# A decode attention kernel with its TensorE program turned into a hardware loop over half heads

## The chip, the cores and the metric

The kernel runs on one core of a Trainium2 chip. The metric is device time in microseconds (us) of one execution. The change was measured with four runs of each kernel.

## The reference, cut to what matters

One token goes through a layer norm, then through attention with 16 query heads over 8 cached key and value heads, and beside it through a small gated feed-forward. The caches decide the cost: 65536 positions of 256 bf16 numbers, for 8 heads, keys and values, are 537 MB.

```python
B, Sq, D = 1, 1, 448
Hq, Hkv, Sk, Dh = 16, 8, 65536, 256
q = (x @ wq) split into 16 heads
scores = einsum("bhqd,bhkd->bhqk", q, k) * Dh ** -0.5      # two query heads per key head
p = softmax(scores);  o = einsum("bhqk,bhkd->bhqd", p, v);  A = o @ wo
# feed-forward: g = silu(x @ w_gate), u = x @ w_up, y = (g * u) @ w_down
out = x + A + (xn + y * sigmoid(r))
```

## The kernel before

Keys and values stream into a ring in SBUF in chunks of 64 positions per partition (128 x 64 x 256 bf16 = 4.19 MB, 32 KB per partition). The ring is a bump allocator: whatever comes next takes the next free stretch, and it also holds all weights. With 84480 elements it holds 5.2 chunks.

```python
RING = 84480
...
K_CHUNKS = [64] * 8
V_CHUNKS = [64] * 8
...
SPREAD = True
...
for n, it in enumerate(items):
    if pos + it["size"] > RING:
        pos = 0
    it["off"] = pos
    # it["need"]: the last earlier item that overlaps this stretch; the issue waits until it is free
...
def prog_sp():                       # one queue issues all loads, in order
    for n, it in enumerate(items):
        for m in range(max(0, it["need"] - 8), it["need"] + 1):
            wait("sp", "pe", ("FREE", m))
        ... nc.sync.dma_start(dst, src).then_inc(sem_it[it["sem"]], 16)
```

For each set of 16 positions TensorE transposes the keys (16 fp32-typed transposes, `ps_t`), VectorE and ScalarE copy them to SBUF, TensorE multiplies them with q (8 matmuls, `ps_q`), and the scores are transposed into place (`ps_s`). When a head is complete, softmax runs and its V chunks are multiplied with the probabilities (`ps_o`). The keys of the next head stream between them.

The gate weights of the feed-forward are loaded with a rearranged source. The rows land on partitions in another order, so a second set of activation columns exists to match.

```python
def flat_dma(src, n, off, spread):
    def d(a):
        dst = a[:, off:off + RP * n // 2]                # 128 partitions
        v = src.rearrange("a b -> (a b)")
        if spread:
            return dst, v.rearrange("(u a n) -> a u n", a=8, u=P // 8)
        return dst, v.rearrange("(p n) -> p n", p=P)
    return d
...
item("ffn1", RP * F, [flat_dma(B_w_gate, F, 0, SPREAD), flat_dma(B_w_up, F, RP * F // 2, False)])
```

The program of every engine is fully written out: TensorE executes 9576 matmuls, each with a weight load, and no branch.

Of the kernel before, what the change touches and what calls it, by code (L numbers as in the profile page):

```python
# [2 lines left out]

# [4 lines left out]
FP32 = mybir.dt.float32  # L8
# [4 lines left out]
RING = 84480  # L13
NSEM = 16
NTB = 4
NKT = 8
K_FIRST = [16, 16, 32] + [64] * 7
K_CHUNKS = [64] * 8
V_CHUNKS = [64] * 8
V_LAST = [64] * 7 + [32, 16, 8, 8]  # L20
SPREAD = True
WO_END = 2
ACT_M = (3,)
TORD = (3, 0, 1, 2)


def bass_parallel_sum__gqa_block_cached__moe_arch_mod__decode_kernel(
# [22 lines left out]
    HR = D // P  # L50
# [6 lines left out]
    NSET = NPP // SETN  # L57
    SBN = 256
    NSB = NPP // SBN
    SETS_PER_SB = SBN // SETN  # L60
    HB = FK // 2
    assert rep == 2 and NH == 2 and NPP % SBN == 0
# [6 lines left out]
    OROWS = 32 * (NG - 1) + 2 * rep  # L69

# [7 lines left out]
    ring = S_("ring", [P, RING], BF16)  # L78
    kt_buf = [S_(f"kt_buf{i}", [P, 8 * P], BF16) for i in range(NKT)]
    s2 = [S_(f"s2_{i}", [P, 512], BF16) for i in range(2)]  # L80
    S_sb = [S_(f"S_sb{i}", [P, NPP, rep], BF16) for i in range(2)]
    ident_bf = S_("ident_bf", [P, P], BF16)
# [6 lines left out]
    xe_row = S_("xe_row", [1, 2, 2, NE, P], BF16)  # L89
    xnT_sb = S_("xnT_sb", [P, 2, 2 * NE + 2 * (NE - 1)], BF16)  # L90
    qT_sb = S_("qT_sb", [P, NH, Hq], BF16)
    m1p = S_("m1p", [P, 2, rep, NSB], FP32)
    m1 = S_("m1", [P, 2, rep], FP32)
    gmax = S_("gmax", [rep, 1], FP32)
    diag = S_("diag", [rep, rep], FP32)
    negmax = S_("negmax", [P, Hkv, rep], FP32)
    rowsum = S_("rowsum", [P, Hkv, rep], FP32)
    rs = S_("rs", [P, Hkv, NH, rep], FP32)
# [4 lines left out]
    oT_sb = S_("oT_sb", [P, 2, NH, rep], BF16)  # L103
# [18 lines left out]
    ps_tf = [t[:, :].bitcast(FP32) for t in ps_t]  # L122
    ps_q = PS_("ps_q", [P, 512], FP32)
# [8 lines left out]
    sems = []  # L132

    def SEM(name):
        s = nc.semaphore(name)
        sems.append(s)
        return s.__enter__()

    sem_prog = {e: SEM(f"prog_{e}") for e in ("pe", "act", "dve", "pool")}
    sem_it = [SEM(f"sem_it{i}") for i in range(NSEM)]  # L140
    sem_w0 = SEM("sem_w0")
    sem_out = SEM("sem_out")
# [3 lines left out]
    class Ctx:  # L146
        emit = False
        ev = {e: {} for e in sem_prog}
        cnt = {e: 0 for e in sem_prog}
        waited = {}  # L150
        tasks = {"dve": [], "act": []}

    ctx = Ctx()

    def mark(e, key, ins):
        ctx.cnt[e] += 1
        c = ctx.cnt[e]
        if ctx.emit:
            assert ctx.ev[e][key] == c, (e, key, ctx.ev[e][key], c)
            ins.then_inc(sem_prog[e], 1)  # L160
        else:
            assert key not in ctx.ev[e], (e, key)
            ctx.ev[e][key] = c
        return c
# [5 lines left out]

    def wait(we, e, key):
        if not ctx.emit:
            return
        c = ctx.ev[e][key]
        k = (we, e)
        if ctx.waited.get(k, 0) >= c:
            return
        ctx.waited[k] = c
        engines[we].wait_ge(sem_prog[e], c)

    def wait_val(we, sem, val, key):
        if not ctx.emit:
            return
        k = (we, key)
        if ctx.waited.get(k, 0) >= val:
            return
        ctx.waited[k] = val
        engines[we].wait_ge(sem, val)

    def op(e, key, fn):  # L190
        mark(e, key, fn(engines[e]) if ctx.emit else None)
# [6 lines left out]
    items = []  # L198

    def item(kind, size, dmas, **kw):  # L200
        items.append(dict(kind=kind, size=size, dmas=dmas, **kw))
        return len(items) - 1

    def flat_dma(src, n, off, spread):
        def d(a):
            dst = a[:, off:off + RP * n // 2]
            v = src.rearrange("a b -> (a b)")
            if spread:
                return dst, v.rearrange("(u a n) -> a u n", a=8, u=P // 8)
            return dst, v.rearrange("(p n) -> p n", p=P)  # L210
        return d

    def kv_item(kind, src, h, n0, J):
        def d(a):
            return (a[:, 0:J * Dh].rearrange("p (j d) -> p j d", d=Dh),
                    src[0, h].rearrange("(p n) d -> p n d", p=P)[:, n0:n0 + J, :])
        return item(kind, J * Dh, [d], h=h, n0=n0, J=J)

    def wo_item(h):
        def d(a):  # L220
            return (a[:, 0:rep * NH * D].rearrange("p (i f n) -> p i f n", i=rep, f=NH),
                    A_wo[h * rep * Dh:(h + 1) * rep * Dh, :].rearrange("(i p f) n -> p i f n", i=rep, f=NH))
        return item("wo", rep * NH * D, [d], h=h)

    def head_chunks(kind, src, h, sizes):
        r, n = [], 0
        for J in sizes:
            r.append((kind, src, h, n, J))
            n += J
        assert n == NPP  # L230
        return r

    item("wq", RP * HqDh // 2, [flat_dma(A_wq, HqDh, 0, False)])
    ks = head_chunks("k", A_k_cache, 0, K_FIRST)
    for h in range(1, Hkv):
        ks += head_chunks("k", A_k_cache, h, K_CHUNKS)
    vs = []
    for h in range(Hkv):
        vs += head_chunks("v", A_v_cache, h, V_CHUNKS if h < Hkv - 1 else V_LAST)

    def v_next():
        v = vs.pop(0)
        if v[3] + v[4] == NPP and v[2] < Hkv - WO_END:
            wo_item(v[2])
        kv_item(*v)
        if v[2] == 0 and v[3] == 2 * V_CHUNKS[0]:
            item("ffn1", RP * F, [flat_dma(B_w_gate, F, 0, SPREAD), flat_dma(B_w_up, F, RP * F // 2, False)])
        if v[2] == 0 and v[3] == 3 * V_CHUNKS[0]:
            item("ffn2", FK * D, [lambda a: (a[:, 0:FK * D].rearrange("p (f n) -> p f n", f=2),
                                             B_w_down.rearrange("(f p t) n -> p f (t n)", p=P, f=2))])  # L250

    for n, k_ in enumerate(ks):
        kv_item(*k_)
        if n >= len(K_FIRST) + 1:
            v_next()
    while vs:
        v_next()
    for h in range(Hkv - WO_END, Hkv):
        wo_item(h)



    pos = 0
    live = deque()
    semtot = [0] * NSEM
    for n, it in enumerate(items):
        if pos + it["size"] > RING:
            pos = 0
        it["off"] = pos
        lo, hi = pos, pos + it["size"]  # L270
        need = n - NSEM
        for m in list(live):
            o = items[m]
            if o["off"] < hi and lo < o["off"] + o["size"]:
                need = max(need, m)
        while live and live[0] <= need:
            live.popleft()
        live.append(n)
        it["need"] = need
        pos = hi  # L280
        s = n % NSEM
        semtot[s] += 16 * len(it["dmas"])
        it["sem"], it["val"] = s, semtot[s]
        assert it["size"] <= RING

    def ap_of(n):
        it = items[n]
        return ring[:, it["off"]:it["off"] + it["size"]]

    def wait_item(we, n):  # L290
        it = items[n]
        wait_val(we, sem_it[it["sem"]], it["val"], ("it", it["sem"]))

    def free_item(n):
        alias("pe", ("FREE", n), ctx.cnt["pe"])

    def prog_sp():
        for n, it in enumerate(items):
            for m in range(max(0, it["need"] - 8), it["need"] + 1):
                wait("sp", "pe", ("FREE", m))  # L300
            for d in it["dmas"]:
                if ctx.emit:
                    dst, src = d(ap_of(n))
                    nc.sync.dma_start(dst, src).then_inc(sem_it[it["sem"]], 16)  # L304
        wait("sp", "dve", ("RES", Hkv - 1))
        if ctx.emit:
            nc.sync.dma_start(out[0], res_bf[:, :]).then_inc(sem_out, 16)
            nc.sync.wait_ge(sem_out, 16)

    def prog_pool():  # L310
# [23 lines left out]
        alias("pool", "CONST", ctx.cnt["pool"])  # L334


    st = dict(slot=0, m=[], pend_qk=None, pend_jt=None)
    deferred = deque()

    def slot():  # L340
        st["slot"] += 1
        if deferred and deferred[0][0] <= st["slot"]:
            deferred.popleft()[1]()

    def defer(after, fn, tag=None):
        deferred.append((st["slot"] + after, fn, tag))

    def flush():
        while deferred:
            deferred.popleft()[1]()  # L350

    def evac_T(e, g):
        wait(e, "pe", ("T", g))
        if g >= NKT:
            wait(e, "pe", ("QK", (g - NKT) // NG))
        kt, tb = kt_buf[g % NKT], ps_t[g % NTB]
        if e == "dve":
            op(e, ("EV", g), lambda x: x.tensor_copy(out=kt[:, :], in_=tb[:, :]))  # L358
        else:
            op(e, ("EV", g), lambda x: x.activation(out=kt[:, :], in_=tb[:, :], func=ACTF.Copy))  # L360

    def ev_engine(m):
        return "act" if m in ACT_M else "dve"

    def pe_T(n, s, m, j):

        g = s * NG + m
        if g >= NTB:
# [524 lines left out]
```

## Time and profile before

| | before |
|---|---|
| median of runs, first three / all four | 1312.85 / 1312.37 us |
| bytes read | 549 MB |
| rate in most slices | 430 GB/s |
| 549 MB at 430 GB/s | 1277 us |
| TensorE busy | 922.5 us, 70% |

First the page of the kernel before: the busy times with their share of the span, the rate in 40 equal slices of 32.8 us, and the DMA queues with their packets.

```profile
span 1310.5 us, 20912 instructions
...
PE 922.5 (70%) x9576; PEld 694.6 (53%) x9576; DVE 539.0 (41%) x895; ACT 432.4 (33%) x559; POOL 4.5 (0%) x34
...
GB/s 400 430 430 430 384 335 433 431 427 432 431 430 429 429 430 429 431 429 431 431 431 431 428 430 430 431 430 429 428 430 429 431 423 430 430 430 431 431 430 205
...
q1 hardware_dynamic: 22026, 549.04, 98.5%
q8 instruction: 75, 1.23, 0.4%
...
```

The first slice, the fifth and sixth and the last fall well short of 430 GB/s; the others stay within 2% of it. `q8` is instruction fetch: 75 packets of 16 KB, 1.23 MB, a fifth of a per cent of the bytes.

The table of waits, its line for TensorE and the K chunks (total us, times, longest):

```profile
...
PE ps_t L374 <- DMA ring<-in_A_k_cache_dram: 300.3, 55, 8.8
...
```

TensorE waits 300 us for keys, so the DMA is the limit.

The next view cuts the span into stretches around the gate load. Each line gives the stretch, its length, and each engine's busy time with its count of instructions; the last three columns are granted TensorE clock (as a share of full speed), busy share of the 16 DMA engines, and GB/s.

```profile
...
core 0: us, PE busy (x) PEld busy (x) DVE busy (x) ACT busy (x) POOL busy (x), PEclk, DMA share, GB/s
148.00:156.00 8.00, 4.80 (x29) 3.88 (x30) 2.08 (x3) 1.06 (x2) 0.00 (x0) 0.63 1.03 442
156.00:164.00 8.00, 7.98 (x84) 6.45 (x84) 5.28 (x9) 4.78 (x6) 0.00 (x0) 0.95 0.97 224
164.00:172.00 8.00, 1.90 (x32) 0.67 (x32) 0.39 (x1) 1.88 (x2) 0.00 (x0) 0.91 1.09 236
172.00:180.00 8.00, 0.00 (x0) 0.00 (x0) 0.00 (x0) 0.00 (x0) 0.00 (x0) 0.50 0.94 260
180.00:188.00 8.00, 5.32 (x98) 5.30 (x98) 0.00 (x0) 0.00 (x0) 0.00 (x0) 0.50 0.98 421
...
```

From 156 to 180 us the DMA engines are as busy as ever and move little more than half. The packets' own durations in the trace say how: 12544-byte packets (gate and up) take 0.94 us, and 0.47 us once it is over; the 32 KB packets of the caches that run at the same time take 2.34 us on average instead of 1.22.

The same view at the end:

```profile
...
1284.00:1292.00 8.00, 2.99 (x32) 0.80 (x24) 0.00 (x0) 0.00 (x0) 0.00 (x0) 0.71 0.83 343
1292.00:1300.00 8.00, 4.62 (x48) 1.24 (x48) 0.00 (x0) 0.00 (x0) 0.00 (x0) 0.69 0.35 137
1300.00:1308.00 8.00, 5.32 (x28) 1.31 (x28) 0.85 (x2) 0.00 (x0) 0.00 (x0) 0.52 0.08 32
...
```

The DMA engines run out one after the other: the busy share is 0.35 and then 0.08. From 1296 to 1305 us it is about 0.13, that is about two engines of 16 (0.13 x 16 = 2.1).

The last steps in the timeline (start, duration, engine, line):

```profile
...
1303.50 0.60 PE L694 MATMUL ps_o<-ring,S_sb 128*4 128x512 bf16 x4 [0.66 <-DMA ring<-in_A_v_cache_dram]
1304.90 0.27 PE L534 MATMUL ps_m<-sel_bf,ob_sb 100*128 100x2 bf16 x4 [0.80 <-DVE ob_sb L514]
1305.10 3.15 PE L562 MATMUL ps_s<-ring,oT_sb 128*1 128x448 bf16 x8
```

After the last four V matmuls only the output projections of the last two heads remain, and the span ends 7.0 us after they start.

One more table is needed; it comes from the trace's records of semaphore increments. For every whole chunk it holds 16 increments, at different times and as many as the page counts DMA engines; I read each as the landing of one engine's part. Listed is how many us before the last one each of the 16 came, for one item near the given time.

```
before,  254 us:  0.0 0.4 1.3 2.4 3.2 3.4 3.6 3.7 7.6 8.2 8.2 8.3 8.3 8.3 10.6 11.0
before, 1274 us:  0.0 1.2 7.8 8.6 8.7 9.3 9.4 9.5 9.6 12.3 14.9 15.2 15.2 15.5 19.0 19.5
```

The engines drift apart, and the kernel waits for the last of them.

### The profile page before, as it was taken

To read this page: it belongs to the slowest core of one execution; us is meant where nothing else is said; L and a number is where in the kernel's file an instruction comes from. 1 tells how busy PE (TensorE), PEld (TensorE's weight loads), DVE (VectorE), ACT (ScalarE), POOL (GpSimd) and SP (SyncE) were. 2 spreads that over 40 slices of the span, in tenths; PEclk is the share of its full clock that TensorE was granted. 3 is DMA by queue.
4 is the path that set the end of the run, shared out by engine and by line. 5 is a ranking of instruction groups with operands and counts; after the bars stand their busy time and mean duration, and the time that the engine had idled before them with its cause. 6 is when DMAs were issued, how large, how long until landed. Compare 5 with 4: busy or idle time off the path is not lost.

```text
span 1310.5 us, 20912 instructions
## 1 busy us (share of the span) xinstructions
PE 922.5 (70%) x9576; PEld 694.6 (53%) x9576; DVE 539.0 (41%) x895; ACT 432.4 (33%) x559; POOL 4.5 (0%) x34
## 2 busy tenths in 40 slices
PE   4998837768668577677677677577676686786534
PEld 4886625546546456455555556455465565565201
DVE  5776404444344344344343354344343353453200
ACT  2665303333233233233233243233332342332100
POOL 1000000000000000000000000000000000000000
PEclk9999768888888788787887888888887887888756
DMA  9999999999999999999999999999999999999994
GB/s 400 430 430 430 384 335 433 431 427 432 431 430 429 429 430 429 431 429 431 431 431 431 428 430 430 431 430 429 428 430 429 431 423 430 430 430 431 431 430 205
DMA packets 22117, 550.37 MB, mean 420 GB/s; under 512 B 2315, under 2 KB 4366, under 8 KB 4878
## 3 DMA queue, kind: packets, MB, share of 16 engines
q1 hardware_dynamic: 22026, 549.04, 98.5%
q8 instruction: 75, 1.23, 0.4%
q14 instruction: 12, 0.10, 0.0%
q10 hardware_dynamic: 4, 0.00, 0.0%
HBM read 549.03 MB, written 0.00 MB: 419 GB/s over the span
## 4 chain that ended last, share of the span: by engine, by line
DMA 73%; PE 26%; another core or an unknown queue 1%; SPq 0%; issue 0%; DVE 0%
DMA ring<-in_A_k_cache_dram 66%; PE ps_t L374 18%; DMA ring<-in_A_v_cache_dram 6%; PE ps_q L401 4%; PE ps_o L694 2%; PE ps_s L434 1%; PE ps_m L579 0%; SPq L304 0%; PE ps_m L644 0%; PE ps_s L562 0%; PE ps_m L534 0%; PE ps_m L505 0%; DVE ob_sb L514 0%; DVE res_bf L547 0%
## 5 line engine op out<-in xcount | busy, mean ns | idle before, releaser
L374 PE MATMUL ps_t<-ident_f,ring 128*128 128x128 f32 x4096 | 602.3, 310 | 302.1 <-DMA ring<-in_A_k_cache_dram 300.3
L374 PEld LDWEIGHTS ps_t<-ident_f,ring 128*128 128x128 f32 x4096 | 536.2, 161 | 419.1 <-DMA ring<-in_A_k_cache_dram 328.6
L358 DVE COPY kt_buf<-ps_t 128x1024 bf16<-128x1024 bf16 x768 | 492.6, 685 | 629.7 <-PE ps_t L374 628.7
L360 ACT ACTIVATE kt_buf<-ps_t 128x1024 bf16<-128x1024 bf16 x256 | 262.1, 1024 | 430.0 <-PE ps_t L374 429.2
L386 ACT ACTIVATE s<-ps_q 98x512 bf16<-98x512 f32 x256 | 152.9, 597 | 330.2 <-PE ps_q L401 330.2
L401 PE MATMUL ps_q<-kt_buf,qT_sb 128*2 128x512 bf16 x2048 | 173.5, 417 | 0.0
L694 PE MATMUL ps_o<-ring,S_sb 128*4 128x512 bf16 x2048 | 136.0, 410 | 48.9 <-DMA ring<-in_A_v_cache_dram 46.9
L694 PEld LDWEIGHTS ps_o<-ring,S_sb 128*4 128x4 bf16 x2048 | 50.7, 88 | 121.9 <-DMA ring<-in_A_v_cache_dram 54.9
L434 PEld LDWEIGHTS ps_s<-sel_bf,s 128*128 128x128 bf16 x1024 | 67.8, 102 | 7.6 <-ACT s L386 1.6
L434 PE MATMUL ps_s<-sel_bf,s 128*128 128x8 bf16 x1024 | 64.8, 169 | 0.7 <-ACT s L386 0.7
L514 DVE CAST ob_sb<-ps_o 100x512 bf16<-100x512 f32 x8 | 5.5, 692 | 83.2 <-PE ps_o L694 83.2
L401 PEld LDWEIGHTS ps_q<-kt_buf,qT_sb 128*2 128x2 bf16 x2048 | 26.3, 79 | 5.6 <-issue 0.2
L607 PE MATMUL ps_m<-xnT_sb,ring 128*128 128x2 bf16 x210 | 8.5, 179 | 18.0 <-DMA ring<-in_B_w_up_dram 16.4
L607 PEld LDWEIGHTS ps_m<-xnT_sb,ring 128*128 128x128 bf16 x210 | 8.4, 127 | 18.6 <-DMA ring<-in_B_w_up_dram 16.9
L480 ACT ACTIVATE S_sb<-S_sb,negmax 128x512 bf16<-128x512 bf16 x16 | 13.4, 863 | 5.3 <-DVE negmax L473 5.3
L414 DVE CAST S_sb<-ps_s 128x512 bf16<-128x512 f32 x16 | 10.9, 681 | 1.3 <-PE ps_s L434 1.3
L416 DVE TENSOR_REDUCE m1p<-S_sb 128x2 f32<-128x512 bf16 x16 | 11.0, 686 | 0.6
L592 DVE TENSOR_TENSOR gs_sb<-ps_m,sg_sb 128x14 f32<-128x14 f32 x1 | 0.2, 173 | 23.9 <-ACT sg_sb L587 23.9
L708 PE MATMUL ps_m<-ident_bf,xe_row 1*128 1x1 bf16 x16 | 0.6, 161 | 12.9 <-DVE xe_row L822 12.9
L505 PEld LDWEIGHTS ps_m<-rowsum,ones_f 128*128 128x128 f32 x32 | 5.5, 246 | 6.0 <-issue 6.0
L587 ACT ACTIVATE sg_sb<-ps_m 128x14 f32<-128x14 f32 x1 | 0.2, 184 | 22.2 <-PE ps_m L607 22.2
L708 PEld LDWEIGHTS ps_m<-ident_bf,xe_row 1*128 1x128 bf16 x16 | 0.5, 100 | 12.9 <-DVE xe_row L822 12.9
(67 smaller groups left out, 73.7 us busy)
## 6 DMA issues: line engine op xcount, KB each, us to landing
ring<-in_A_k_cache_dram SPq DMA_DIRECT2D x63, 4096.0 KB, 44.1
ring<-in_A_v_cache_dram SPq DMA_DIRECT2D x63, 4096.0 KB, 37.3
ring<-in_A_wq_dram SPq DMA_DIRECT2D x1, 3584.0 KB, 11.4
ring<-in_A_wo_dram SPq DMA_DIRECT2D x8, 448.0 KB, 29.2
ring<-in_A_k_cache_dram SPq DMA_DIRECT2D x2, 1024.0 KB, 13.4
ring<-in_A_k_cache_dram SPq DMA_DIRECT2D x1, 2048.0 KB, 20.6
ring<-in_A_v_cache_dram SPq DMA_DIRECT2D x1, 2048.0 KB, 41.6
ring<-in_B_w_gate_dram SPq DMA_DIRECT2D x1, 1568.0 KB
```

The costliest lines, as they stand in the source:

```text
L358: op(e, ("EV", g), lambda x: x.tensor_copy(out=kt[:, :], in_=tb[:, :]))
L360: op(e, ("EV", g), lambda x: x.activation(out=kt[:, :], in_=tb[:, :], func=ACTF.Copy))
L374: ins = nc.tensor.matmul(ps_tf[g % NTB][:, jj * P:(jj + 1) * P], lhsT=kv[:, j + GN * m + jj, :], rhs=ident_f[:, :], is_transpose=True, sta ...
L386: op("act", ("EVQ", s), lambda e: e.activation(out=s2[s % 2][0:QROWS, :], in_=ps_q[0:QROWS, :], func=ACTF.Copy))
L401: ins = nc.tensor.matmul(ps_q[32 * m:32 * m + rep, 0:512], lhsT=qT_sb[:, hf, h * rep:(h + 1) * rep], rhs=kt[:, :].rearrange("p (k f) -> p ...
L414: op("dve", ("SCOPY", b), lambda e: e.tensor_copy(out=S[:, k * SBN:(k + 1) * SBN, :], in_=ps_s[:, :, :]))
L416: op("dve", ("SMAX", b), lambda e: e.tensor_reduce(out=m1p[:, h % 2, :, k], in_=S[:, k * SBN:(k + 1) * SBN, :].rearrange("p n i -> p i n") ...
L434: ins = nc.tensor.matmul(o, lhsT=s2[s % 2][:, jj * P:(jj + 1) * P], rhs=sel_bf[:, :, :], start=True, stop=True)
L480: op("act", ("EXPI", h, i), lambda e, i=i: e.activation(out=S[:, :, i], in_=S[:, :, i], func=ACTF.Exp, bias=negmax[:, h, i:i + 1], scale=1 ...
L505: ins = nc.tensor.matmul(ps_m[0:P, C_TOT + f * rep:C_TOT + (f + 1) * rep], lhsT=ones_f[:, :], rhs=rowsum[:, h, :], start=True, stop=True)
L607: ins = nc.tensor.matmul(o, lhsT=cols(a, rr * width, c), rhs=X[:, x0:x0 + 2], start=(b == 0), stop=(b == RP * half - 1), skip_group_check= ...
L694: ins = nc.tensor.matmul(ps_o[32 * g:32 * g + 2 * rep, :], lhsT=S[:, k:k + 2, :].rearrange("p n i -> p (n i)"), rhs=kv[:, j:j + 2, :], sta ...
```

## The change

The intent is to turn TensorE's program into a loop. One turn handles half a head: four K chunks of half head t+2, four V chunks of half head t. For one set of instructions to serve all 14 turns, every address must repeat:

- the ring becomes four fixed slots of 32 KB, and a turn uses each twice; weights move to areas of their own (`w_area`, `wo_cur`);
- q of the current head and the probabilities are copied to fixed places (`q_cur`, `p_sb`) by ScalarE;
- waits in the loop compare semaphores with registers that grow by a fixed step each turn;
- softmax statistics and the output projection are done per half head, some of it without use, so that all turns are alike.

Two things come along. The gate load loses its rearranged source and moves to the start. `w_down` and the last output projection weights are now loaded behind the last V chunk.

```diff
-RING = 84480
+NSLOT = 4
+CH = 64
+ORDER = [("k", 0), ("v", 0), ("k", 1), ("v", 1), ("k", 2), ("v", 2), ("v", 3), ("k", 3)]
-SPREAD = True
...
-    ring = S_("ring", [P, RING], BF16)
+    ring = S_("ring", [P, NSLOT * SLOT], BF16)
+    w_area = S_("w_area", [P, WQN], BF16)
+    wo_cur = S_("wo_cur", [P, WON], BF16)
+    p_sb = S_("p_sb", [P, HC, CH, rep], BF16)
+    q_cur = S_("q_cur", [P, NH, rep], BF16)
...
+    item("wg", w_area[:, 0:WGN], [flat_src(B_w_gate, 0, F), flat_src(B_w_up, WGN // 2, F)], "wg", [("QT",)])
...
+    def act_pc(t, c):
+        op("act", ("PC", t, c), lambda e: e.activation(out=p_sb[:, c, :, :], in_=S_sb[t // 2 % 2][:, n:n + CH, :], func=ACTF.Copy), "pc")
...
+            for v in loop_regs():
+                ctx.regs[v] = e.alloc_register(f"w{v[0]}_{v[1]}")
+                e.reg_mov(ctx.regs[v], v[0])
+            with e.Fori(0, NT):
+                turn(False)
+                for (v0, step), r in ctx.regs.items():
+                    e.reg_add(r, r, step)
...
+        pe_oT(NT + 1)
+        pe_ffn2()
+        wait_item("pe", "wo_end")
+        mark("pe", ("ATTN", NT + 1), attn_mm(ps_fin, items["wo_end"]["ap"]))
```

## The prediction

> **What bounds the kernel now.** The DMA queue. The page counts 549 MB read at 430 GB/s in most slices: 1277 us of a 1310.5 us span. TensorE is 70% busy and waits 300 us for K chunks (table of waits); the chain of waits is 73% DMA. TensorE is slower than the DMA only where K chunks come alone: four sets take 4 x 2.54 = 10.15 us (timeline) against 9.74 us per 4.19 MB.
>
> 33 us are to be had, mostly in three places.
> 1. The gate weights. From 156 to 178 us the windows show 200 to 240 GB/s with the DMA engines fully busy: 12.5 KB packets take 0.93 us (0.47 later), K packets 2.4 us instead of 1.22. SPREAD makes that load's source 8 x 16, its destination 128. [...] By landings on the slowest DMA engine, the five items around it (20.0 MB, 46.5 us at 430 GB/s) took 60.9 us: 14.4 us lost.
> 2. Skew. After that the slowest two DMA engines land each chunk 8 to 11 us after the fast ones, at the end up to 19 us; from 1296 to 1305 us the DMA share is 0.13, two engines of 16. Instruction fetches (75 pages of 16 KB, one each 17 us, about 0.6 us of an engine) add about 7 us to the slowest engine.
> 3. The tail from the last data to the end, 1305 to 1310.5 us.
>
> **What the change does.**
> - It drops SPREAD: gate and up load as wq does, at full rate. About -14 us, the main term, directly on the critical path.
> - Ring from 5.2 chunks to 4. A freed slot is requested 10 to 13 us after landing; the slowest engine then has 3 x 9.74 - 13 = 16 us queued. No starvation.
> - ACT gets 64 copies of 128x128 and 16 of q, by estimate 15 to 25 us on an engine 33% busy; on the path once per head, where V waits for exp and a copy, about 4 us, hidden behind 16 us of queue. Cost 0.
> - The loop: the same 9576 matmuls with 14 branches. If the turn (by count some 1400 instructions, 6 pages) stays in instruction memory, most fetches vanish (up to -7 us). If each branch fetches anew, fetches may double (+5 to +10 us). I take -1.
> - The tail: w_down and the last wo now follow the last V chunk, and ffn2 (14 matmuls at 0.37 us) precedes the last projection. Last V to end was 7 us; estimate 3.7 + 5 + 1.5 + 3 = 13 us, with 5 instead of 2.3 us of bytes behind V: +3.5 us.
>
> Sum: 1312.85 - 14.4 + 3.5 - 1 = 1301 us; 80% range 1288 to 1311. Chances: faster by over 2% 0.08, within 2% 0.88, slower 0.04.
>
> **What would show each step.** No slice under 420 GB/s but the first and last; 12.5 KB packets near 0.47 us. The DMA share stays 0.9. Instruction queue: packets far under 75, or 100 and more. Timeline of the end: ffn2 after the last V matmul..
>
> **What would make it wrong.** Branch stalls beyond 15 us per turn, or register waits that slow TensorE past 19.5 us per K and V pair: slower. All fetches and the skew gone: below 1290. Slots starving the DMA at each head: around 1320.

The 14.4 us come from the landings alone, and the sum stays 1312.85 - 14.4 + 3.5 - 1 = 1301 us (1300.95). The 0.6 us and 7 us for fetches are estimates. The 0.6 us is worked out from the K packets (32 KB in 1.22 us), the 7 us is not worked out there; fetch packets in before are recorded at 1.01 to 1.11 us but for one of 1.32, and with 60 fewer fetches the same work was later measured 7.9 us faster (`r5_after_again` against `e3_unrolled`). The "6 pages" follow from before's 19248 recorded TensorE instructions for 75 fetches, 257 each. That a turn "stays in instruction memory", here and in `e3_unrolled`, can be seen only as missing fetch packets: none between 174.3 and 1218.7 us in after.

## The result, and the profile after

| | before | after |
|---|---|---|
| median us (four runs each) | 1312.37 | 1292.66 |
| lowest to highest | 1310.19 to 1312.99 | 1292.09 to 1293.12 |
| ratio | | 0.9853, 95% interval 0.9835 to 0.9870 |

A ratio is the mean time of one kernel's runs over that of the other's of the same rounds, so it is not quite the ratio of the medians. The gain is 1.5%; it is clear of noise. The prediction was 1301 us, with 1288 to 1311 as its range.

The same lines of the page:

```profile
span 1291.1 us, 21412 instructions
...
PE 934.6 (72%) x9673; PEld 669.9 (52%) x9673; DVE 551.6 (43%) x944; ACT 446.5 (35%) x634; POOL 4.5 (0%) x34
...
GB/s 404 425 433 424 431 432 430 432 429 431 435 428 434 428 434 432 428 435 426 435 433 429 435 427 432 431 432 435 424 436 429 434 431 427 436 429 434 429 431 243
...
q1 hardware_dynamic: 22034, 549.04, 99.1%
q8 instruction: 15, 0.25, 0.1%
...
```

No slice between the first and the last is below 424 GB/s, and the instruction queue has 15 packets instead of 75. In the trace none of them falls between about 175 and 1219 us, in which time TensorE takes 13 branches back to the loop's start (recorded at 0.2 us each). One turn holds 1196 recorded TensorE instructions, on average. That fits a body that is fetched once: before has 19248 recorded TensorE instructions and 75 fetches, 257 each; after has 2856 outside the loop and 1196 in it, which at 257 each would be 15.8 fetches.

TensorE and the keys:

```profile
...
PE ps_t L382 <- DMA ring<-in_A_k_cache_dram: 217.1, 43, 7.7
...
```

TensorE still waits for the DMA, though less: 217 us, and 98 us more for V.

The gate and up load, whose packets now run from 50 to 59 us:

```profile
...
44.00:52.00 8.00, 8.00 (x90) 6.54 (x88) 5.78 (x10) 5.18 (x7) 0.00 (x0) 1.00 0.95 403
52.00:60.00 8.00, 8.00 (x90) 6.53 (x89) 6.05 (x10) 5.17 (x7) 0.00 (x0) 1.00 1.04 443
60.00:68.00 8.00, 6.04 (x71) 4.50 (x69) 5.15 (x9) 3.86 (x6) 0.00 (x0) 1.00 1.02 436
...
```

There is no dip, and its 12544-byte packets take 0.48 us.

The end:

```profile
...
1268.00:1276.00 8.00, 5.46 (x48) 1.39 (x48) 0.00 (x0) 0.00 (x0) 0.00 (x0) 0.50 0.98 403
1276.00:1284.00 8.00, 3.88 (x24) 0.93 (x25) 0.86 (x2) 0.00 (x0) 0.00 (x0) 0.50 0.26 107
1284.00:1291.00 7.00, 4.86 (x15) 1.55 (x13) 1.28 (x2) 0.00 (x0) 0.00 (x0) 0.71 0.00 0
...
```

The engines run out closer together: the low stretch is 8 us long instead of 16. The last 7 us move no data at all. The timeline says what is done in them:

```profile
...
1278.84 0.60 PE L541 MATMUL ps_o<-ring,p_sb 128*4 128x512 bf16 x4 [0.66 <-DMA ring<-in_A_v_cache_dram]
...
1282.60 5.39 PE L656 MATMUL ps_t<-w_area,hT_sb 128*1 128x448 bf16 x14 [2.10 <-DMA w_area<-in_B_w_down_dram]
...
1287.78 1.08 PE L593 MATMUL ps_s<-w_area,oT_sb 128*1 128x448 bf16 x4
...
1288.90 0.61 DVE L663 TENSOR_TENSOR res_bf<-ps_s,rowsf 1x448 bf16<-1x448 f32 x1 [0.20 <-PE ps_s L593]
1289.54 0.33 SPq L331 DMA_DIRECT2D out_dram<-res_bf  x1
```

The last V matmuls start at 1278.84 us and the span ends 12.3 us later, 5.3 us more than before. `w_down` (waited for until 1282.60 us) and its 14 matmuls stand in between.

The landing table:

```
after,   247 us:  0.0 0.1 0.3 0.3 1.1 1.3 1.6 1.7 1.8 2.0 3.2 3.3 3.3 3.4 3.4 3.4
after,  1269 us:  0.0 3.4 3.7 3.9 4.2 4.3 4.4 4.5 4.5 6.2 7.0 7.5 7.7 7.8 7.9 7.9
```

The spread was 19.5 us and is 7.9 us.

### The profile page after: what moved, and what is told of

Same layout as the page of the kernel before. It is cut to its first block, busy times and chain, and to the rows that moved or that the text cites. A ratio compares the mean times of both kernels' runs of the same rounds, so it can differ in the third digit from the quotient of the medians.

```text
span 1291.1 us, 21412 instructions
## 1 busy us (share of the span) xinstructions
PE 934.6 (72%) x9673; PEld 669.9 (52%) x9673; DVE 551.6 (43%) x944; ACT 446.5 (35%) x634; POOL 4.5 (0%) x34
## 4 chain that ended last, share of the span: by engine, by line
DMA 76%; PE 22%; DVE 1%; ACT 0%; issue 0%; SPq 0%; ACTq 0%
DMA ring<-in_A_k_cache_dram 42%; DMA ring<-in_A_v_cache_dram 31%; PE ps_t L382 13%; PE ps_o L541 4%; PE ps_q L416 3%; DMA w_area<-in_B_w_down_dram 3%; DMA wr_row<-in_B_w_r_dram 0%; PE ps_s L449 0%; PE ps_t L656 0%; PE ps_m L624 0%; DVE kt_buf L370 0%; ACT S_sb L494 0%; SPq L328 0%; PE ps_m L593 0%; ACT L494 0%
## 5 line engine op out<-in xcount | busy, mean ns | idle before, releaser
L382 PE MATMUL ps_t<-ident_f,ring 128*128 128x128 f32 x4096 | 578.0, 299 | 218.5 <-DMA ring<-in_A_k_cache_dram 217.1
L382 PEld LDWEIGHTS ps_t<-ident_f,ring 128*128 128x128 f32 x4096 | 502.9, 154 | 343.6 <-DMA ring<-in_A_k_cache_dram 238.5
L541 PE MATMUL ps_o<-ring,p_sb 128*4 128x512 bf16 x2048 | 158.4, 462 | 108.6 <-DMA ring<-in_A_v_cache_dram 98.4
L416 PE MATMUL ps_q<-kt_buf,q_cur 128*2 128x512 bf16 x2048 | 169.0, 407 | 0.7 <-ACT s L394 0.7
L541 PEld LDWEIGHTS ps_o<-ring,p_sb 128*4 128x4 bf16 x2048 | 52.2, 95 | 203.1 <-issue 144.9
L485 ACT ACTIVATE p_sb<-S_sb 128x128 bf16<-128x128 bf16 x64 | 17.1, 303 | 101.7 <-PE ps_o L541 101.5
L416 PEld LDWEIGHTS ps_q<-kt_buf,q_cur 128*2 128x2 bf16 x2048 | 26.2, 79 | 6.9 <-ACT s L394 1.2
L593 PE MATMUL ps_m<-wo_cur,oT_sb 128*1 128x448 bf16 x56 | 15.4, 406 | 0.0
L585 DVE TENSOR_TENSOR rowsf<-ps_m,rowsf 1x448 f32<-1x448 f32 x14 | 8.6, 612 | 4.6 <-PE ps_m L593 4.3
L521 PE MATMUL ps_m<-rowsum,ones_f 128*128 128x2 f32 x60 | 9.9, 270 | 0.0
```

What stands on the lines that cost most here:

```text
L382: ins = nc.tensor.matmul(ps_tf[m][:, jj * P:(jj + 1) * P], lhsT=kv[:, j + GN * m + jj, :], rhs=ident_f[:, :], is_transpose=True, start=Tru ...
L416: ins = nc.tensor.matmul(ps_q[32 * m:32 * m + rep, 0:512], lhsT=q_cur[:, hf, :], rhs=kt[:, :].rearrange("p (k f) -> p f k", f=NH)[:, hf, : ...
L485: op("act", ("PC", t, c), lambda e: e.activation(out=p_sb[:, c, :, :], in_=S_sb[t // 2 % 2][:, n:n + CH, :], func=ACTF.Copy), "pc")
L521: ins = nc.tensor.matmul(ps_m[0:P, C_TOT + f * rep:C_TOT + (f + 1) * rep], lhsT=ones_f[:, :], rhs=rowsum[:, :], start=True, stop=True)
L541: ins = nc.tensor.matmul(ps_o[32 * g:32 * g + 2 * rep, :], lhsT=p_sb[:, c, o + j:o + j + 2, :].rearrange("p n i -> p (n i)"), rhs=kv[:, j: ...
L593: ins = nc.tensor.matmul(dst, lhsT=oT_sb[:, hf, i:i + 1], rhs=wo[:, i, hf, :], start=(hf == 0 and i == 0), stop=(hf == NH - 1 and i == rep ...
```

## The experiments

The change mixes four things that could each matter: the gate load, the loop, the ring, and the new order at the end. The theory was that the gate load is worth 14 us and the loop's missing fetches the rest, less a longer tail. The rivals were that the gate load had been hidden, that the loop as such is worth nothing, or that the smaller ring takes some of the gain back. Each timed run had five rounds. The times of one table come from one chip.

| run | median us | ratio to before (95%) |
|---|---|---|
| before | 1310.27 | |
| `e1_flat_gate` | 1298.18 | 0.9905 (0.9890 to 0.9920) |
| `e2_flat_gate_ring4` | 1308.22 | 0.9979 (0.9965 to 0.9993) |
| `e3_unrolled` | 1300.02 | 0.9920 (0.9907 to 0.9934) |
| `e4_double_body` | 1301.74 | 0.9934 (0.9921 to 0.9948) |

| run | median us | ratio to before (95%) |
|---|---|---|
| before | 1311.50 | |
| `r5_after_again` | 1292.17 | 0.9856 (0.9841 to 0.9871) |
| `e5_after_split_gate` | 1308.15 | 0.9974 (0.9958 to 0.9990) |
| `e6_gate_16x8` | 1305.18 | 0.9957 (0.9943 to 0.9970) |
| `e7_early_down` | 1290.80 | 0.9847 (0.9834 to 0.9861) |

| run | median us | ratio to before (95%) |
|---|---|---|
| before | 1310.00 | |
| `e8_ring4_own_wo` | 1299.15 | 0.9914 (0.9899 to 0.9928) |
| `r6_flat_gate_again` | 1297.99 | 0.9906 (0.9890 to 0.9923) |

### The gate load alone, in before

```diff
-SPREAD = True
+SPREAD = False
```

> The kernel before, with only the gate load changed: laid out flat as the up load is (128 partitions on both sides), with the first set of activation columns. Theory: the split gate load cost the slowest DMA engine 14.4 us, all on the path, so 1298 us (1296 to 1301), no slice below 420 GB/s around 130 to 200 us, packets of 12544 B near 0.47 us, landing skew below 5 us at 250 us; instruction fetches stay at 75, and the skew grows afterwards by 6 to 9 us. Rival: the load was mostly hidden and the whole gain came from the loop: 1308 to 1313 us.

Measured: 1298.18 us, correct. The dip is gone. The rate line of its page, and the instruction queue:

```profile
...
GB/s 404 430 426 431 425 432 432 427 430 431 431 427 432 431 429 432 429 427 430 431 431 429 431 433 426 429 434 425 431 432 430 431 429 428 432 428 433 431 429 247
...
q8 instruction: 75, 1.23, 0.4%
...
```

The landings of the slowest engine give the size. The five items around the gate load took 60.9 us in before and take 46.7 us here: 14.2 us less. The next 117 items, to the last whole V chunk, took 1091.2 us in before and take 1091.4 us here. So the load cost what it seemed to cost, and nothing of it was given back. The landing spread grows again, from 4.8 us at 251 us to 15.9 us at 1270 us, by 11 us and not by the 6 to 9 expected. It ends in two groups of eight:

```
flat gate, 1270 us:  0.0 0.1 1.1 1.3 1.5 1.7 1.7 1.8 9.0 12.6 14.9 15.5 15.5 15.5 15.7 15.9
```

The rival (gain from the loop only) is out. Once more, this kernel ran in 1297.99 us:

> The flat gate kernel again, on the same chip as the run with its own place for the projection weights: 1297 to 1299 us.

### The gate load split again, in after

```diff
-    item("wg", w_area[:, 0:WGN], [flat_src(B_w_gate, 0, F), ...
+    item("wg", w_area[:, 0:WGN], [(lambda a: a[:, 0:WGN // 2], B_w_gate.rearrange("a b -> (a b)").rearrange("(u a n) -> a u n", a=8, u=P // 8)), ...
```

> The kernel after, with the gate load split 8 x 16 at its source again (the activation columns are not rearranged to match, so the result is wrong on purpose). Theory: the split load costs the slowest DMA engine about 14 us wherever it stands: 1305 to 1309 us. Rival: early in the program the cost is hidden in the start: below 1296 us.

Measured: 1308.15 us, and a wrong result. After itself ran in 1292.17 us with 16 fetches (15 had been expected):

> The kernel after unchanged, so that the runs sent with it have it on the same chip: 1292 to 1294 us, 15 instruction fetches.

The split costs 16.0 us here. By landings it is all in the start: the slowest engine lands the eighth K chunk of the program at 115.2 us instead of 98.7 us (`r5_after_again`), and needs the same 1141 us for the stretch after it. So the split load costs about as much at the start as in the middle of the program, where it cost 14.2 us. The windows around it:

```profile
...
44.00:52.00 8.00, 8.00 (x90) 6.51 (x89) 6.04 (x11) 5.06 (x7) 0.00 (x0) 1.00 1.03 357
52.00:60.00 8.00, 7.91 (x94) 6.36 (x95) 5.89 (x10) 4.82 (x6) 0.00 (x0) 1.00 1.02 162
60.00:68.00 8.00, 5.61 (x64) 4.11 (x61) 4.73 (x8) 3.79 (x5) 0.00 (x0) 1.00 1.08 175
68.00:76.00 8.00, 0.00 (x0) 0.00 (x0) 0.00 (x0) 0.00 (x0) 0.00 (x0) 0.53 0.90 339
...
```

The DMA engines are fully busy at 162 to 175 GB/s.

### Why the split load is slow

The load's semaphore hints at how many engines carry it. The kernel raises it by 16 for each load, so by 32 for gate and up together. In after the trace has 32 increments for them. In before it has 25: one at 130.6 us, right after the gate load was issued (129.42 us, 0.78 us long) and before the first packet of either load (156.8 us), and 24 from 165.2 us on. In `e5_after_split_gate` there are 25 too. If the 24 are single steps, the early one stands for 8, and 16 for the up load leave 8 for the gate load. So I read that 8 engines carry the split load, an inference from this count.

That would explain half the engines, but not why the cache packets slow down too (2.34 us instead of 1.22). To tell the two apart, the source was split 16 x 8, still in strides, to bring in all 16 engines:

```diff
-            return dst, v.rearrange("(u a n) -> a u n", a=8, u=P // 8)
+            return dst, v.rearrange("(u a n) -> a u n", a=16, u=P // 16)
```

> The kernel before, with the gate load split 16 x 8 instead of 8 x 16 (result wrong on purpose). If it is the number of DMA engines, 8 instead of 16, that makes the load slow, the time falls as with the flat load, to 1297 to 1301 us, and 12544 B packets take near 0.47 us. [...]packets stay slow (above 0.7 us) and the time stays above 1304 us.

Measured: 1305.18 us (wrong result), all 16 engines by the count of increments (16 single steps for the gate load), and packets of 0.85 us. Two stretches around the load:

```profile
...
156.00:164.00 8.00, 7.55 (x84) 6.01 (x84) 5.66 (x9) 5.17 (x7) 0.00 (x0) 1.00 0.97 212
164.00:172.00 8.00, 1.90 (x32) 0.67 (x32) 0.00 (x0) 1.48 (x2) 0.00 (x0) 0.85 1.01 254
...
```

By landings the five items around the load take 54.7 us here, against 60.9 us with the 8 x 16 split and 46.7 us flat. So the 16 x 8 split wins back about 6 of the 14.2 us, and 8 us of loss remain although, by that count, all 16 engines take part: the number of engines is not the whole cause. Per packet, 16 engines are nearly as slow (0.85 us on average over all gate and up packets, 0.89 us in before, 0.48 us flat).

What slows the two split forms is not shown. They share a source in strides: neighbouring partitions take stretches of the source that lie 8 or 16 places apart, where the flat form takes them in order. No run here varied the reads or the writes alone. What is shown is that both split forms are slow (0.89 and 0.85 us per packet) and the flat form is not (0.48 us).

### The loop, undone

```diff
+        elif UNROLL:
+            for t in range(NT):
+                half(t)
         else:
             def turn(collect):
...
-        wait_sem(we, *ctx.ev[e][key])
+        if key in ctx.ev[e]:
+            wait_sem(we, *ctx.ev[e][key])
```

This is the kernel after with its 14 turns written out and constant waits; all else is unchanged.

> The kernel after, with its 14 turns written out instead of looped: same ring, same order, same copies, constant waits. Theory: the loop's gain is that its instructions stay in instruction memory, so written out the fetches come back (70 to 85 pages of 16 KB instead of 15) and slow the slowest DMA engine by 6 to 8 us: 1299 to 1301 us, landing skew at the end 10 us or more. Rival: fetches are harmless and the loop is worth nothing, or register waits and branches even cost: 1290 to 1294 us.

Measured: 1300.02 us, correct. Its instruction queue:

```profile
...
q8 instruction: 76, 1.25, 0.4%
...
```

The loop is worth 1300.02 - 1292.17 = 7.9 us by the medians; from the ratios, 0.9920 / 0.9856 is 0.65%, or 8.4 us. By landings of the slowest engine, the stretch from the eighth K chunk to the V chunk that fills the fourth slot for the 31st time takes 1140.9 us in after and 1148.8 us written out. Its bytes at 430 GB/s would take 1139 us. So the looped kernel has almost nothing left to gain there, and the difference is again 7.9 us.

The landing spread at 1267 us is 12.7 us, again in two groups of eight:

```
unrolled, 1267 us:  0.0 0.2 0.7 1.7 2.0 2.1 2.2 2.2 8.3 11.4 11.7 12.3 12.4 12.6 12.6 12.7
```

Eight of the 16 engines fall behind where there are fetches (by 8.3 to 12.7 us here), and in after, with three fetches between 247 and 1269 us, the whole spread grows only from 3.4 to 7.9 us. The trace does not name a packet's engine, so which engines carry the fetches is not shown. If the 60 more fetches fell evenly on the eight late ones, that would be 7.5 each, and 7.9 us over 7.5 is 1.05 us of delay per fetch, an estimate that rests on this "if". It lies close to the 1.02 to 1.10 us that most such packets are recorded with, but the match may be chance, because the slowest engine of after, with which it compares, is itself held back by something else (see "Open"). In the flat-gate run the eight late engines fall behind the eight early ones by 10.1 us on average between 261 and 1250 us, in which there are 57 fetches: 1.4 us each, by the same reckoning. So 7.9 us for the whole is measured; the share of one fetch is not settled.

### A loop body twice as long

```diff
-            with e.Fori(0, NT):
-                turn(False)
-                for (v0, step), r in ctx.regs.items():
-                    e.reg_add(r, r, step)
+            with e.Fori(0, NT // 2):
+                for _ in range(2):
+                    turn(False)
+                    for (v0, step), r in ctx.regs.items():
+                        e.reg_add(r, r, step)
```

> The kernel after, with two half heads in one loop turn and 7 turns: same work, twice the instructions in the loop body (about 2800 of 64 B, 11 pages). In before the first fetch came when TensorE had used up about one page[...]. Theory: the body no longer fits, each turn fetches about 11 pages again, 77 or more in all, and the time goes to 1299 to 1303 us. Rival: looped code is kept whatever its length: 15 fetches and 1292 to 1294 us.

The 64 B follow from before: 16 KB a fetch over 257 recorded TensorE instructions. The first fetch there starts at 20.2 us, when 281 of them are recorded.

Measured: 1301.74 us, correct. Its instruction queue:

```profile
...
q8 instruction: 86, 1.41, 0.4%
...
```

There is still a loop, but 86 fetches, more than written out, and no gain. One turn holds up to 2394 recorded instructions. So it is not looping that helps but a body that need not be fetched again: one of 1196 instructions is not, one of 2394 is. The expectation of 1299 to 1303 us held.

This run has a second loss, though. Each of its six taken branches is recorded at 6.0 to 6.6 us in place of 0.2, and TensorE stands still for it. The timeline just after the branch at 747 us:

```profile
...
753.35 3.65 PE L382 MATMUL ps_t<-ident_f,ring 128*128 128x128 f32 x16 [5.50 <-issue]
...
```

A window 11 us later, in which the DMA share falls to 0.81:

```profile
...
764.00:772.00 8.00, 7.04 (x86) 4.79 (x79) 3.66 (x10) 5.66 (x13) 0.00 (x0) 1.00 0.81 328
...
```

So the 9.6 us between this run and after can be fetch traffic and branch stalls together, and no run separates the two. The run written out has no branches, and is the one that gives the 7.9 us.

### The ring of four, in before

```diff
-RING = 84480
+RING = 65536
```

on top of the flat gate load.

> The same as the run before it, with the ring cut from 84480 to 65536 elements, that is four chunks of 32 KB in place of 5.2. Theory: after a slot is freed the slowest DMA engine still has about 16 us queued, so the cut costs nothing: within 1.5 us of the flat gate run. Rival: the cut costs DMA time at the head changes or at the start: 5 us or more slower, with slices below 420 GB/s.

This went against the theory: 1308.22 us, 10.0 us more than with the large ring. Its rate falls once per head. The rate line, and windows at one such place:

```profile
...
GB/s 400 431 431 430 423 400 426 431 397 432 433 432 429 393 432 429 430 429 389 432 432 432 430 413 432 431 427 429 397 432 432 431 426 397 431 431 428 431 433 322
...
```

```profile
...
444.00:448.00 4.00, 4.00 (x29) 3.07 (x28) 2.08 (x3) 1.02 (x1) 0.00 (x0) 0.50 0.99 426
448.00:452.00 4.00, 4.00 (x42) 3.10 (x43) 2.61 (x5) 2.22 (x3) 0.00 (x0) 0.98 0.42 180
452.00:456.00 4.00, 4.00 (x48) 3.42 (x50) 2.95 (x6) 2.62 (x3) 0.00 (x0) 1.00 1.04 385
...
```

From 448 to 452 us the DMA engines are busy for 42% of the time. By landings the 117 items after the gate load take 1101.3 us instead of 1091.4 us, which is the whole loss. The idle place comes after a load of output projection weights: they also take a stretch of the ring, and beside them only three chunks fit. The remedy tried was to give them two places of their own:

```diff
-        if pos + it["size"] > RING:
+        if it["kind"] != "wo" and pos + it["size"] > RING:
             pos = 0
-        it["off"] = pos
+        own = it["kind"] == "wo"
+        it["off"] = RING + it["h"] % WO_END * WON if own else pos
```

> The flat gate kernel with the ring cut to 65536 elements, but with the projection weights in two places of their own beside it, so that each of the four chunk places holds only K or V. In the ring of four before, the DMA engines stood idle once per head where the projection weights took ring space. Theory: that was the whole cost, so the time is that of the flat gate run with the large ring, 1297 to 1300 us, and no slice falls to 390 to 400 GB/s. Rival: four places are too few at the change of heads: 1304 us or more.

Measured: 1299.15 us (1297.89 to 1299.38) against 1297.99 us for the large ring, ratios 0.9914 and 0.9906. The 117 items take 1091.4 us again. No slice is as low as in the ring of four before, where they fell to 389; two fall short, with 408 and 419 GB/s, where "no slice falls to 390 to 400" had been expected. Four whole chunks are enough, three and some weights are not.

### A shorter tail

In after, `w_down` and `wo_end` go before the last two V chunks, and ffn2 before the last V chunk:

```diff
     for t in range(NT, NT + 2):
         for c in range(HC):
+            if t == NT + 1 and c == 2:
+                item("wd", ...);  item("wo_end", ...)
             v_slot(t, c, ...)
...
+                if t == NT + 1 and c == 2:
+                    pe_ffn2()
         pe_oT(NT + 1)
-        pe_ffn2()
```

> The kernel after, with w_down and the last projection weights loaded before the last two V chunks and ffn2 done between them, so that after the last V matmul only the evacuation, the projection and the output are left. Theory: data end to kernel end was 7.3 us in after and becomes 5 to 6, so 1 to 2.5 us faster than after: 1290 to 1292 us. Rival: the tail is hidden by something else and the time is that of after.

Measured: 1290.80 us (1290.18 to 1291.59), correct, against 1292.17 us (1291.73 to 1292.71) for after. The ranges do not touch; the intervals of the two ratios to before overlap, since before itself varied by 4 us. The timeline of its end:

```profile
...
1283.65 0.39 PE L542 MATMUL ps_o<-ring,p_sb 128*4 128x512 bf16 x4 [0.85 <-DMA ring<-in_A_v_cache_dram]
1284.09 0.69 DVE L558 CAST ob_sb<-ps_o 100x512 bf16<-100x512 f32 x1 [2.46 <-PE ps_o L542]
...
1285.35 1.28 PE L594 MATMUL ps_s<-w_area,oT_sb 128*1 128x448 bf16 x4 [0.25 <-DVE oT_sb L567]
1286.67 0.61 DVE L664 TENSOR_TENSOR res_bf<-ps_s,rowsf 1x448 bf16<-1x448 f32 x1 [1.38 <-PE ps_s L594]
1287.31 0.32 SPq L332 DMA_DIRECT2D out_dram<-res_bf  x1
```

The last V matmuls start at 1283.65 us and the span of 1288.8 us ends 5.2 us later, instead of 12.3. V itself lands later, since the same bytes now come before it, so most of the 7 us is not gained, only 1.4 us. This is the fastest version found.

## Why the prediction was right or wrong

**The bound (right).** The DMA bounds both kernels. Of the 33.5 us of the span of before above the 1277 us of bytes, the gate load (14.2), the loop's term (7.9) and the stretch after the last V matmuls begin (7.0) make about 29.

**The gate load, "about -14 us, the main term" (right).** 14.2 us by landings in before; 12.1 us by medians, 1.0% by the ratio; 16 us when put into after. Why the load is slow was not shown. Measured are 25 increments in place of 32, read as 8 engines, and 8 us of loss that stay with 16 engines.

**The loop, "I take -1" (the step that was mis-sized).** It measured -7.9 us. The prediction named two outcomes, fetches gone "up to -7 us" and fetches doubled "+5 to +10 us", and took a value near their middle. The first came true: 15 fetches instead of 75. The cost of one fetch was also undersized, since a fetch was put down at 0.6 us of an engine, from 16 KB at the rate of the K packets, when the page's own packets are mostly recorded at 1.02 to 1.10 us; the runs give 1.05 to 1.4 us of delay per fetch by estimate, if eight engines share them, which no trace shows. The durations stood in the trace of before and had not been used. This term accounts for 6.9 of the 8.3 us between 1301 and 1292.66 us; most of the rest is the tail, put at +3.5. That the result still lies in the stated range owes something to the width of that range, 23 us, which had to hold both outcomes of the loop.

**The ring, "No starvation" (right for the kernel after, for a reason the prediction left out).** The sum of 16 us still queued holds only where the four slots hold nothing but chunks. With the same size and weights in it, before with the flat gate lost 10 us. The "10 to 13 us" are in after, between 250 and 1230 us, 2.1 to 15.1 us from the last landing in a slot to the issue of its next load (median 9.6); by the same reckoning at least 3 x 9.74 - 15.1 = 14 us stay queued, an estimate. What protects the kernel after is that `wo` moved to a place of its own in the same change.

**Copies on ScalarE, "Cost 0" (agrees, not isolated).** ScalarE was busy 14 us more on the page (432.4 to 446.5), a little below the estimate of 15 to 25. TensorE waited 10.2 us in all for the copies into `p_sb` before V matmuls (8 waits, the longest 2.3 us). The matmuls are not quite the same 9576 either, but 9673, since all turns are alike. The unrolled kernel has the copies, the ring, the half heads and the new tail, and is 1.8 us slower than before with a flat gate. All of that together costs 1.8 us, less than the tail was expected to cost alone.

**The tail, "+3.5 us" (right in kind).** From the last V matmul to the end: 13 us predicted, 12.3 measured, 7.0 before. The 14 matmuls of ffn2 took 5.39 us in after, 0.385 us each, against 0.37 predicted. The run that shortens it gains 1.4 us. What the tail costs against before was not measured alone; the 1.8 us above includes it.

**Sum.** From 1312.4 us: gate -14.2, loop -7.9, the rest +1.8, gives 1292.1; measured 1292.66. The gate term is taken from the landings here, because the median of before moved between 1310.0 and 1312.4 us; with the 12.1 us of the medians the sum would be 1294.2.

**Open.** After 620 us one engine of after falls behind all others in steps of up to 1 us, about 200 us apart, to 3.4 us at 1269 us (3.8 in `r5_after_again`), with no instruction fetch until 1219 us. Its cause was not looked for.

## What to carry to other kernels

When a kernel is bound by DMA, read the landings of the single DMA engines and not only the mean rate: here a load with an unlucky split cost 14.2 us, and 1 MB of instruction fetches, 0.2% of the bytes, cost 7.9 us. A hardware loop on the engine with the longest program paid here by ending its instruction fetches (15 instead of 75, 7.9 us); twice that body gained nothing (86 fetches, 1301.74 us). When a ring is cut to "n slots", count what else lives in it.
